# Three list changes at the start of an attention and MLP kernel: pair 7's transposes ahead of unit 5's pieces, unit 10's load behind layer norm's transposes, the first values' casts behind unit 1's keys

## The chip, the cores and the metric

One core of a Trainium2 chip. The metric is device time in microseconds (us) of one execution; most executions of a kernel here agree within 0.3%.

## The reference

Eight batches, 12 heads, 448 rows, head size 64; the attention's output goes through layer norm and an MLP.

```python
q_n, k_n = rmsnorm(q, g_q), rmsnorm(k, g_k)          # over the 64 columns of a head
attn = softmax(q_n @ k_n.T / 8)                      # 448 x 448 per head
x = (attn @ v) as [8, 448, 768]
xn = layernorm(x) * g_ln
out = x + relu(xn @ w_ch1) @ w_ch2                   # 768 -> 3072 -> 768
```

## The kernel before

Heads are worked in pairs (six per batch), and pairs are prepared in units: units 0 and 1 hold one pair, all others two. A unit's preparation is cut into lettered pieces: `a` and `c` square keys and queries (ScalarE), `d` and `e` sum the squares (VectorE), `i`, `j`, `k`, `l`, `m` make the float16 keys `khl` (high and low halves) and queries `qn`, `z` casts the values. Up to unit 7, TensorE then transposes a pair's keys and queries (`K`, `Q`); from unit 8 on this is done by transposing DMA transfers on SyncE's queue (`x`, `y`). Scores are `S`, products with the values `V`, layer norm's transposes `X`.

Batch 0's start is a hand-made list:

```python
ORDER = """
G b0 a0 c0 L4 L5 i0 j0 e0 k0 gq0 l0 b1 m0 a1 c1 K0 Q0 d0 gk0 S0.0 S0.1 i1 e1 d1 z0 g1 j1 l1 m1
k1 b2 ...                                            # cut
S6.6 V6.4 X0 X1 U0 N2 d5 j5 R X2 c5 e5 g5 k5 z5 l5 L7 V6.5 U1 U2 M m5 V6.6
""".split()
DMA_UNIT = 8
```

Everything after it is spread over steps of attention, and the load of unit u + 2 is listed one step behind the last of unit u's evenly spread pieces (step `e`):

```python
            if u < nu - 2 and f"L{u + 2}" not in done:
                todo.setdefault(e + 1, []).append(lambda u=u: self.load_unit(u + 2))
```

What turns out to matter is where a unit's `khl` and `qn` live. They come from a pool with two buffers of each, and the square's result is parked in the same buffer before the keys are made in it:

```python
        self.p_n = pool("p_n", 2)
        ...
            c["qn"] = self.p_n.tile([128, 14, 2, D], FP16, tag="qn", name="qn")[:, 0:g]
            c["khl"] = self.p_n.tile([128, 14, 2, D], FP16, tag="khl", name="khl")[:, 0:g]
        ...
        def square(n):
            o = c["khl" if n == 1 else "qn"].rearrange("p g e d -> p (g e d)").bitcast(FP32)
            ...
            nc.scalar.activation(c["sq", n], c["t"][n], AFT.Square)
        ...
        def dma_k():                                 # from unit 8 on; dma_q likewise reads qn
            nc.sync.dma_start_transpose(
                kU[:, 0:1536].rearrange("p (g c) -> p g c", c=128), khl[:, 0:12])
```

Which of the two buffers a unit gets is not written here; it is settled when the kernel is built.

Of the kernel before, what the change touches and what calls it, by code (L numbers as in the profile page):

```python
# [33 lines left out]


ORDER = """
G b0 a0 c0 L4 L5 i0 j0 e0 k0 gq0 l0 b1 m0 a1 c1 K0 Q0 d0 gk0 S0.0 S0.1 i1 e1 d1 z0 g1 j1 l1 m1
k1 b2 a2 S0.2 d2 c2 S0.3 S0.4 K1 V0.0 e2 i2 S0.5 Q1 g2 l2 S0.6 S1.0 j2 V0.1 S1.1 S1.2 m2 b3
V0.2 a3 V0.3 k2 c3 S1.3 K2 V0.4 S1.4 z2 V0.5 Q2 V0.6 V1.0 S1.5 i3 W0 d3 e3 S1.6 V1.1 V1.2 S2.0
j3 T0 V1.3 S2.1 S2.2 Q3 V1.4 S2.3 K3 S2.4 V1.5 V1.6 S2.5 g3 z3 S2.6 V2.0 S3.0 S3.1 V2.1 k3  # L40
# [1 line left out]
V3.2 d4 i4 K5 W1 c4 W2 V3.3 V3.4 V3.5 V3.6 S4.2 S4.3 V4.0 S4.4 S4.5 V4.1 e4 j4 T1 S4.6 S5.0 k4  # L42
g4 V4.2 V4.3 V4.4 V4.5 S5.1 l4 S5.2 S5.3 K6 V4.6 S5.4 z4 m4 b5 V5.0 S5.5 V5.1 G2 L6 V5.2 S5.6
V5.3 V5.4 V5.5 Q6 a5 i5 V5.6 T3 S6.0 S6.1 S6.2 S6.3 T5 S6.4 A V6.0 V6.1 N0 V6.2 N1 V6.3 S6.5
S6.6 V6.4 X0 X1 U0 N2 d5 j5 R X2 c5 e5 g5 k5 z5 l5 L7 V6.5 U1 U2 M m5 V6.6
""".split()
DMA_UNIT = 8
PE_SET = (DMA_UNIT + 1) % 2
# [27 lines left out]
class _Fast:  # L76
# [381 lines left out]
    def attention(self):  # L458

        n, nu, nb0, done = B * NPAIR, len(UNITS), NPAIR, set(ORDER)  # L460
        todo, last = {}, -9
        for u in range(4, nu):
            p, m = UNIT_PAIR[u], UNITS[u][2]
            st = max(7 * (p - 2 - m) + 2, last + 1, 7 * nb0)
            e = max(7 * (p - 2) - 1, st + 5)
            st, e = EARLY.get(u, (st, e))
            pieces = ["bai", "d", "c", "e", "j", "gv", "k", "l", "m", "w", "x", "y"]
            k = len(pieces) - 2
            if u < DMA_UNIT:
                pieces = pieces[:k]  # L470
            if f"z{u}" in done and u == 4:
                continue
            if u < nu - 2 and f"L{u + 2}" not in done:
                todo.setdefault(e + 1, []).append(lambda u=u: self.load_unit(u + 2))
            last = e
            for x, names in enumerate(pieces):
                at = st + (e - st) * x // (k - 1) if x < k else e + 1 + x - k
                todo.setdefault(at, []).extend(
                    self.prep_ops(u)[y] for y in names
                    if not {y + str(u), f"z{u}" if y in "vw" else ""} & done)  # L480
                if u in (6, 7) and x == 0:
                    todo[at].append(lambda u=u: self.load_w2(u - 6))
        steps, mark = [], [0]

        for p in range(nb0, n + 1):
            for i in range(7):
                c = []
                if i == 0 and p < n and p % NPAIR == 0 and p > nb0:
                    c.append(lambda b=p // NPAIR: self.batch(b))
                c += todo.pop(7 * p + i, [])  # L490
                if p < n and f"S{p}.{i}" not in done:
                    c.append(lambda p=p, i=i: self.scores(p, i))
                if p > nb0:
                    for x in {0: (), 1: (0, 1)}.get(i, (i,)):
                        if f"V{p - 1}.{x}" not in done:
                            c.append(lambda p=p, x=x: self.values(p - 1, x))
                if p > nb0 + 1 and i == 1 and (p - 1) % NPAIR:
                    c.append(lambda p=p: self.stats(p - 2))
                if p + 1 < UNIT_PAIR[DMA_UNIT]:
                    if i == 2 and f"K{p + 1}" not in done:  # L500
                        c.append(lambda p=p: self.trans_k(p + 1))
                    if i == 4 and f"Q{p + 1}" not in done:
                        c.append(lambda p=p: self.trans_q(p + 1))
                if p > nb0 and p % NPAIR == 0 and i == 6:
                    c.append(lambda p=p: self.stats(p - 1))
                if c:
                    steps.append(c)
            if p > nb0 and p % NPAIR == 0:
                mark.append(len(steps))
        return steps, mark  # L510
# [416 lines left out]
```

## Time and profile before

| | before |
|---|---|
| time, median of 3 runs | 615.03 us (614.38 to 616.64) |
| span of the profiled run, granted clock | 613.8 us, 0.996 |
| TensorE busy | 581.6 us (95%) |
| first matmul group of batch 1's MLP (`psH`, 512 columns) | 128.75 us |

In a timeline line the first number is the start in us, the second the busy time, then engine, source line, operation, output and inputs, shapes and count; in brackets stand the engine's idle time just before and what ended it. The prediction shows the lines that it rests on. First ScalarE's timeline of the kernel before at unit 9's two squares:

```profile
110.31 0.95 ACT L215 ACTIVATE khl<-qkv 128x896 f32<-128x896 f32 x1 [1.37 <-PE tr L316]
...
112.72 0.95 ACT L215 ACTIVATE qn<-qkv 128x896 f32<-128x896 f32 x1 [0.42 <-PE tr L330]
```

They are released by TensorE's transposes of pair 13 (unit 7), so unit 9 sits in unit 7's buffers (in the built program the keys of both units stand at address 126848). Then TensorE's timeline of the same stretch, whose only listed gaps from 100 to 128 us are these two:

```profile
111.83 0.35 PE L352 MATMUL psS<-qU,kU 128*128 128x448 f16 x1 [0.27 <-ACT E L358]
...
114.25 0.35 PE L355 MATMUL psS<-qU,kU 128*128 128x448 f16 x1 [0.28 <-ACT E L358]
```

### The profile page before, as it was taken

The numbers are of one execution on the slowest core, as the hardware profiler recorded it, in microseconds if no ns is written. First come the engines' busy times: TensorE is split into PE (matmuls) and PEld (weight loads), VectorE is DVE, ScalarE is ACT, GpSimd is POOL, SyncE is SP. The second block draws the span as 40 slices with busy tenths as digits, with TensorE's granted clock in tenths as the row PEclk, the third lists the DMA queues.
The fourth block names the chain that finished last, engine by engine and source line by source line (L and its number), as shares of the span: only waits on it lengthen the run. The fifth ranks groups of instructions, "written<-read, shape, count | busy, mean of one in ns | idle before, by whom it ended". The sixth has DMA issues, their size and how long they took to land.

```text
span 613.8 us, 11526 instructions
## 1 busy us (share of the span) xinstructions
PE 581.6 (95%) x4500; PEld 346.8 (57%) x4500; DVE 287.2 (47%) x614; ACT 361.4 (59%) x696; POOL 190.1 (31%) x245
## 2 busy tenths in 40 slices
PE   2887999999999999999999999999999999999995
PEld 1555566645566666655566666655566666654564
DVE  5799567823356355643346355642355322440011
ACT  6897886438754498538755398537765377114200
POOL 3844422223452245514453145615322000000000
PEclk9999999999999999999999999999999999999998
DMA  9999899655756477748646496937523330030011
GB/s 213 276 182 229 167 222 204 119 158 122 121 109 126 115 124 152 179 108 143 114 101 140 107 135 151 173 108 149 121 57 87 91 61 2 27 104 0 1 52 56
DMA packets 130861, 75.29 MB, mean 123 GB/s; under 512 B 96656, under 2 KB 121040, under 8 KB 130800
## 3 DMA queue, kind: packets, MB, share of 16 engines
q1 hardware_dynamic: 114048, 45.12, 35.8%
q0 software_dynamic: 16080, 28.94, 21.5%
q8 instruction: 37, 0.61, 0.4%
q10 hardware_dynamic: 672, 0.43, 0.2%
q14 instruction: 24, 0.20, 0.1%
HBM read 52.36 MB, written 11.01 MB: 103 GB/s over the span
## 4 chain that ended last, share of the span: by engine, by line
PE 84%; DMA 5%; DVE 5%; ACT 3%; SPq 1%; issue 1%; POOL 0%; DVEq 0%; ACTq 0%; POOLq 0%
PE psH L611 33%; PE psC L627 33%; PE psS L352 8%; PE oA L381 5%; DMA qkv<-in_k_dram 2%; PE oB L383 2%; ACT E L358 2%; DMA hT<-in_k_dram 1%; PE psS L355 1%; PE psS L356 1%; DVE khl L240 1%; DMA hT<-in_q_dram 1%; ACT qn L215 1%; DVE x L398 1%; DVE qn L67 1%
## 5 line engine op out<-in xcount | busy, mean ns | idle before, releaser
L611 PE MATMUL psH<-xnT,w 128*128 128x512 f16 (+1 forms) x1134 | 242.1, 353 | 1.4 <-DMA xnT<-xn 1.1
L358 ACT ACTIVATE E<-psS,rr_all 128x448 f16<-128x448 f32 x336 | 207.0, 635 | 50.2 <-PE psS L352 44.3
L627 PE MATMUL psC<-w,hT 128*128 128x384 f16 (+1 forms) x1368 | 234.6, 323 | 0.0
L613 ACT ACTIVATE hT<-psH 128x512 f16<-128x512 f32 (+1 forms) x189 | 104.1, 551 | 129.2 <-PE psH L611 126.4
L627 PEld LDWEIGHTS <-hT 128*128 128x128 f16 x1368 | 127.7, 98 | 74.3
L611 PEld LDWEIGHTS <-w 128*128 128x128 f16 x1134 | 102.5, 98 | 82.2 <-issue 2.2
L352 PE MATMUL psS<-qU,kU 128*128 128x448 f16 x288 | 101.5, 359 | 9.1 <-ACT E L358 7.0
L381 PEld LDWEIGHTS <-E 128*128 128x128 f16 x1008 | 71.4, 99 | 50.8 <-issue 5.2
L229 POOL TENSOR_TENSOR qkv<-qkv,gprod 128x896 f32<-128x896 f32 x21 | 43.7, 2079 | 97.7 <-ACT khl L215 62.5
L381 PE MATMUL oA<-v,E 128*128 128x65 f16 x864 | 67.5, 195 | 0.9 <-DVE x L398 0.8
L631 DVE SCALAR_TENSOR_TENSOR x<-psC,rs_all,x 128x384 f32<-128x384 f32 x48 | 29.0, 616 | 70.8 <-PE psC L627 70.2
L396 DVE RECIPROCAL rec_all<-oA 128x6 f32<-128x6 f32 x48 | 9.3, 194 | 98.1 <-PE oA L381 98.0
L383 PE MATMUL oB<-v,E 128*128 128x65 f16 x288 | 52.2, 194 | 0.1
L127 POOL DMA_DIRECT2D qkv<-in_k_dram x14 | 11.2, 797 | 131.1 <-ACT E L358 69.2
L218 DVE TENSOR_REDUCE ssq<-khl 128x14 f32<-128x896 f32 (+1 forms) x24 | 25.6, 1065 | 45.6 <-ACT khl L215 45.5
L352 PEld LDWEIGHTS <-kU 128*128 128x128 f16 x288 | 28.3, 99 | 24.2 <-issue 5.9
L218 DVE TENSOR_REDUCE ssq<-qn 128x14 f32<-128x896 f32 (+1 forms) x25 | 26.2, 1047 | 23.0 <-ACT qn L215 22.8
L67 DVE SCALAR_TENSOR_TENSOR qn<-qkv,rq 128x256 f16<-128x256 f32 (+1 forms) x72 | 26.9, 431 | 19.3 <-ACT rq L223 19.3
L383 PEld LDWEIGHTS <-E 128*128 128x128 f16 x336 | 32.7, 97 | 0.5 <-DVE xl L403 0.2
L398 DVE TENSOR_TENSOR x<-oA,rec_all 128x384 f32<-128x384 f32 x48 | 26.8, 558 | 1.7 <-DVE rec_all L397 0.2
L240 DVE TENSOR_TENSOR khl<-qkv,khl 128x896 f16<-128x896 f32 x21 | 22.8, 1084 | 7.9 <-ACT khl L237 7.9
L540 DVE BATCH_NORM_STATS2 stat<-x 128x6 f32<-128x256 f32 x72 | 26.1, 415 | 0.7
(104 smaller groups left out, 449.0 us busy)
## 6 DMA issues: line engine op xcount, KB each, us to landing
out_dram<-x SPq DMA_DIRECT2D x20, 384.0 KB, 2.5
qkv<-in_k_dram POOLq DMA_DIRECT2D x14, 384.0 KB, 3.9
qkv<-in_q_dram POOLq DMA_DIRECT2D x14, 384.0 KB, 5.1
qkv<-in_v_dram POOLq DMA_DIRECT2D x14, 384.0 KB, 6.7
w<-in_moe_w_ch_dram POOLq DMA_DIRECT2D x3, 1536.0 KB, 13.0
w<-in_moe_w_ch_dram POOLq DMA_DIRECT2D x2, 2304.0 KB, 23.7
qkv<-in_k_dram SPq DMA_DIRECT2D x7, 384.0 KB, 5.7
qkv<-in_q_dram SPq DMA_DIRECT2D x7, 384.0 KB, 5.0
```

Of the source, the lines that this page charges most:

```text
L67: nc.vector.scalar_tensor_tensor(out=out, in0=x, scalar=8.0, in1=r.unsqueeze(2).broadcast_to([x.shape[0], g, D]), op0=ALU.mult, op1=ALU.mult)
L218: nc.vector.tensor_reduce(out=c["ssq"][:, n], in_=c["sq", n], axis=AX.X, op=ALU.add)
L229: (nc.vector if u in DVE_KG else nc.gpsimd).tensor_tensor(out=c["t"][1], in0=c["t"][1], in1=sh.gprod.unsqueeze(1).broadcast_to([128, g, D] ...
L352: nc.tensor.matmul(ps[:, 0:S], c["main"][:, ts(i, 128)], q[:, ts(h, S)], start=True, stop=True)
L358: nc.scalar.activation(out=c["E"][:, i], in_=ps[:, 0:S], func=AFT.Exp, scale=self.rr[:, g:g + 1], bias=EXP_BIAS)
L381: nc.tensor.matmul(oA[:, t, cs], E[:, i, ts(t, 128)], rhs, start=(i == 0 and t == 0), stop=(i == 6 and t == 2))
L383: nc.tensor.matmul(oB[:, cs], E[:, i, 320:448], rhs, start=(i == 0), stop=(i == 6))
L398: nc.vector.tensor_tensor(out=x[:, :, 128 * hp:128 * hp + 128].rearrange("p t (e d) -> p t e d", e=2), in0=oA[:, :, :, 0:D], in1=rec[:, 0: ...
L611: nc.tensor.matmul(ps[:, 0:N], sh.w1[:, dc, ts(f, 128)], xnT[:, dc, 0:N], start=(dc == 0), stop=(dc == NDC - 1))
L613: nc.scalar.activation(out=hT[:, f, 0:N], in_=ps[:, 0:N], func=AFT.Relu)
L627: nc.tensor.matmul(ps[:, 0:g[1]], hT[:, f, ts(t, 128)], sh.w2[:, f, cols], start=(f == 0), stop=(f == NFF - 1))
L631: nc.vector.scalar_tensor_tensor(out=x[:, cols], in0=ps[:, 0:g[1]], scalar=self.rs[:, b, t:t + 1], in1=x[:, cols], op0=ALU.mult, op1=ALU.add)
```

## The change

It is meant to take three waits away from the first 128 us: that of unit 1's keys behind the values' casts, that of pair 7's transposes behind unit 5's pieces, and that of layer norm's transposes behind unit 10's load in SyncE's queue.

```diff
-G b0 a0 ... i1 e1 d1 z0 g1 j1 l1 m1
+G b0 a0 ... i1 e1 d1 g1 j1 l1 m1 z0
 ...
-S6.6 V6.4 X0 X1 U0 N2 d5 j5 R X2 c5 e5 g5 k5 z5 l5 L7 V6.5 U1 U2 M m5 V6.6
+S6.6 V6.4 X0 X1 U0 N2 d5 j5 R X2 K7 Q7 c5 e5 g5 k5 z5 l5 L7 V6.5 U1 U2 M m5 V6.6
 ...
-                todo.setdefault(e + 1, []).append(lambda u=u: self.load_unit(u + 2))
+                todo.setdefault(e + (8 if u == DMA_UNIT else 1), []).append(
+                    lambda u=u: self.load_unit(u + 2))
```

More of the change, by code (lines that the diff above doesn't have):

```diff
@@ L36 @@
 ORDER = """
-G b0 a0 c0 L4 L5 i0 j0 e0 k0 gq0 l0 b1 m0 a1 c1 K0 Q0 d0 gk0 S0.0 S0.1 i1 e1 d1 z0 g1 j1 l1 m1
+G b0 a0 c0 L4 L5 i0 j0 e0 k0 gq0 l0 b1 m0 a1 c1 K0 Q0 d0 gk0 S0.0 S0.1 i1 e1 d1 g1 j1 l1 m1 z0
 k1 b2 a2 S0.2 d2 c2 S0.3 S0.4 K1 V0.0 e2 i2 S0.5 Q1 g2 l2 S0.6 S1.0 j2 V0.1 S1.1 S1.2 m2 b3
```

## The prediction

> **What bounds the kernel now.** I read the page first: busy times per engine, then the rows of 40 slices.
>
> ```profile
> PE 581.6 (95%) x4500; PEld 346.8 (57%) x4500; DVE 287.2 (47%) x614; ACT 361.4 (59%) x696; POOL 190.1 (31%) x245
> ...
> PE   2887999999999999999999999999999999999995
> ...
> ACT  6897886438754498538755398537765377114200
> ```
>
> TensorE is busy 581.6 of 613.8 us. Its 32 us of idle time lie almost wholly at the left end. The busy time by stretches (windows) says how much is where: TensorE was busy 4.28 us of the first 17, 28.86 of the 35 up to 52, 7.97 of the 10 up to 62, 62.32 of the 66 up to 128, and 478.21 of the last 486 (nearly all of that idle is the tail after the last matmul). From 128 us on, a stall-free queue of fixed work runs to the end. So whatever brings TensorE to that point earlier comes off the time one for one, and nothing else can. The time is about 128 + 486, and only the 128 is open to this change.
>
> Next, the waits. On POOL's timeline at the start, the first casts of the values hold up the cast of unit 1's keys, since they wait for a load until 13.69:
>
> ```profile
> 13.69 1.15 POOL L285 CAST v<-w 128x768 f16<-128x768 f32 x1 [9.37 <-DMA w<-in_v_dram]
> 14.78 0.64 POOL L291 CAST vl<-w 64x128 f16<-64x128 f32 x2
> 15.48 0.56 POOL L235 CAST khl<-hT 128x448 f16<-128x448 f32 x1
> ```
>
> VectorE and ScalarE then show what hangs on that cast: the subtraction that makes the low half of the keys, TensorE's transpose K1 (17.08), and the next exp, which TensorE is too late for:
>
> ```profile
> 16.08 0.95 DVE L240 TENSOR_TENSOR khl<-hT,khl 128x448 f16<-128x448 f32 x1 [1.93 <-POOL khl L235]
> ...
> 18.64 0.63 ACT L358 ACTIVATE E<-psS,rr_all 128x448 f16<-128x448 f32 x1 [1.80 <-PE psS L352]
> ```
>
> From 18.64 to 52 ScalarE has no gap over 0.7 us (its waits there: 0.39, 0.61, 0.41), so this stage is bound by ScalarE's fixed list of exps and squares, and starts when this wait ends.
>
> The third group is TensorE's own gaps after 58 us, from its timeline:
>
> ```profile
> 57.86 1.14 PE L611 MATMUL psH<-xnT,w 128*128 128x384 f16 x6 [0.34 <-ACT hT L661]
> 61.52 0.22 PE L327 MATMUL tr<-id,qn 128*128 128x128 f16 x1 [1.16 <-DVE kU L318]
> 66.21 0.35 PE L352 MATMUL psS<-qU,kU 128*128 128x448 f16 x1 [0.83 <-ACT E L358]
> 99.82 0.25 PE L381 MATMUL oA<-v,E 128*128 128x65 f16 x3 [0.82 <-DVE x L398]
> 128.75 1.46 PE L611 MATMUL psH<-xnT,w 128*128 128x512 f16 x6 [1.06 <-DMA xnT<-xn]
> ```
>
> The last is the start of batch 1's MLP. SyncE's queue shows why xnT is late: unit 10's load stood in it for 8.7 us for its buffer, then issued until 109.5, and the transposes of unit 8 and LN came behind it:
>
> ```profile
> 103.98 0.37 SPq L127 DMA_DIRECT2D qkv<-in_k_dram  x1
> ...
> 109.57 3.36 SPq L258 DMA_TRANSPOSE kU<-khl  x1
> ...
> 122.08 5.23 SPq L586 DMA_TRANSPOSE xnT<-xn  x4
> ```
>
> **What the Trainium skill says.** "PSUM — Partial Sum Buffer", section Engine vs sequencer instructions: the ScalarE, VectorE and GpSimd queues are strict FIFO. The trace agrees: unit 1's cast started right behind the two value casts, though its inputs were ready at about 12.3 (the ssq reduction that reads the same tile started at 11.70 and took 0.61). "SBUF — State Buffer", section SBUF: two separate sides: GpSimd and a VectorE operation with two SBUF inputs lock a shared port pair, and the later blocks. The trace fits: the subtraction above took 0.95 us beside a POOL copy, against 0.62 for unit 0's same form alone. "TensorE: Matmul & The Clock Gate", Part 1: the clock is halved until about 3.4 us of sustained activity. Here a 448-column score matmul took 0.53 to 0.58 us up to 24 us and 0.35 from 25.8 on. "DMA: Bandwidth & Descriptors", Queues, rings and completion order: each DMA engine goes round between the queues it has work for. Here the weight load on the software queue took 89% of the engines from 48 to 56 us and the SyncE queue 22%, so unit 6's keys landed 11.2 us after issue.
>
> **Part 1, value casts behind unit 1's keys.** Nothing is added; POOL's order becomes key cast, q copy, then the three value casts. The key cast can run at 12.36 to 12.92. VectorE finishes unit 1's qn at 14.15 and subtracts at once, ending between 14.75 and 15.3 (port lock). K1's transposes then start near 15.1 instead of 17.08. The value casts follow the q copy: 14.7 (or 15.25 behind the lock) plus 0.8 for the first, so the first value matmuls can go at about 16.1, just behind K1. The next score comes at 16.4 and its exp at 16.84, when ScalarE is free of the one before, instead of 18.64: 1.8 us. Further on the q reduction ends near 18.0 instead of 19.70, and unit 2's subtraction starts near 20.1 instead of 21.70, as POOL's product for unit 2 cannot move (POOL's sum of work is the same): 1.6 us. From there ScalarE's list carries it. The loads of weights move along, as POOL issues them after its products. I take **-1.6**.
>
> **Part 2, pair 7's transposes (K7, Q7) ahead of unit 5.** Now they stand in the MLP stream; Q7 waits 1.16 us, because VectorE copies K7 out only at 60.81, behind unit 5's five pieces and an evacuation. After, they follow LN's third transpose X2 directly, all through the one PSUM tile `tr`. In the before clock: X2's copy ends at 55.83, so K7 starts 0.85 late; its copy ends near 57.05, so Q7 starts 0.8 late; then V6.5, the first up matmuls until 59.6, and the first psH near 60.3 after a 0.45 wait for ScalarE. The third psH starts at 62.24 against 61.91: **+0.3**. One stall becomes two of similar sum.
>
> But pacing changes too. Without K7 and Q7 two steps of attention are empty and vanish (44 steps instead of 46 in batch 0), so unit 6's pieces start at the first psH instead of the third, and the scores of pair 7 one chunk earlier. ScalarE, which idled 0.46, 0.88 and 2.19 us from 58 to 63, starts its squares sooner. I followed both lists to 66.8 us: the 0.83 stall at 66.21 becomes about 0.5 near 64.6, and TensorE is then ahead by one score (0.19), so **-0.5** from that point. Last, VectorE's list as built has changed near 98 us: pair 9's evacuation now precedes unit 8's subtraction (1.09 us at 97.68), which is what the 0.82 stall at 99.82 waited behind. I count **-0.8** for it and **+0.5** for new waits of this kind that I cannot see in the reshuffled stretch.
>
> **Part 3, unit 10's load behind LN.** SyncE drops 5.5 us of issue and the 8.7 us buffer wait. Unit 8's eight transposes (12.2 us of issue) then end near 111 instead of 122; LN's four issue as their xn arrive (the last ends at 121.83): issued by 123.1, landed 2.55 later at 125.7, while TensorE has work until 127.69. The stall goes: **-1.06**, I count -1.0. The load itself follows the stores, from about 129.5 to 135; unit 10's first piece comes nine steps of some 1.6 us later, near 143, and keys landed in 5.7 us at the median for SyncE. Hidden.
>
> Sum: -1.6 +0.3 -0.5 -0.8 +0.5 -1.0 = -3.1, so 615.03 becomes about **612.0 us**.
>
> **Rivals.** (a) The start's gain is lost again, because the stage to 56 us is bound by transfers: DMA is at 90% or more up to about 60 us, and the weight stream ended at 56.2. For it: those digits. Against: TensorE and ScalarE never waited for a load between 18.6 and 56. If so only parts 2 and 3 count: 613.6. (b) ScalarE, in order, meets unit 6's square before its keys have landed (near 57), or the reshuffled order makes new exp waits; then psH stalls behind it. For it: the pieces come 3 us earlier against a load that took 11.2. Against: by my count the square stands near 60 even with the shift. Cost 1 to 3 us: 613 to 615. (c) The two serial copies in `tr` cost more than the one wait: with VectorE late, K7 and Q7 lose 2.5 instead of 1.65: 612.9. (d) The clock gate opens one window sooner since TensorE starts K1 earlier, saving up to another 1 us: 611. (e) The load of unit 10 is now late for its square: then a wait near 143; I see 5 us of slack.
>
> **Range and chances.** All terms are local and small against 2% (12.3 us). Losing the start's gain and adding one stall of rival b gives 614.4; everything at its best, with d and no new waits, gives 609.8. Range **609.8 to 614.4**. Chances: faster by over 2%: 0.01; within 2%: 0.98; slower: 0.01.
>
> **What will show it.** POOL's first cast is khl near 12.4 and K1 stands near 15.1; the exp at 18.64 is near 16.9 (part 1 right). TensorE shows two gaps of about 0.8 us ahead of K7 and Q7, with none of 1.16 later (part 2). The 0.82 wait for x and the 1.06 wait for xnT are gone, and no psH or square waits for unit 6 or unit 10 (part 3). Batch 1's first psH starts near 125.6 instead of 128.75, and the 486 us behind it are unchanged. I am wrong if that stretch after the first psH of batch 1 changes by more than 0.5 us, or if a new wait over 1 us stands between 52 and 125.

## The result, and the profile after

The changed kernel took 615.17 us (median of 4 runs, 614.83 to 615.97), the kernel before 615.08 us beside it (4 runs, 614.38 to 616.64). The ratio is 1.000, with a 95% interval of 0.9978 to 1.0022: the same, and outside the predicted range of 609.8 to 614.4. A ratio here is the mean time of one kernel's fast runs over that of the other's fast runs of the same rounds, so it is not quite the ratio of the medians quoted.

The three waits did go. Here is the start of the changed kernel, from the timeline of all engines:

```profile
12.71 0.56 POOL L235 CAST khl<-hT 128x448 f16<-128x448 f32 x1 [8.40 <-DVE ssq L218]
...
14.33 0.62 DVE L240 TENSOR_TENSOR khl<-hT,khl 128x448 f16<-128x448 f32 x1
...
15.96 1.87 ACT L358 ACTIVATE E<-psS,rr_all 128x448 f16<-128x448 f32 x3
```

The key cast stands at 12.71 in place of 15.48, the subtraction takes 0.62 in place of 0.95 us (it starts first here, and now the copy of queries on GpSimd that starts beside it takes 0.89 us in place of 0.56), and the exp that waited 1.80 us at 18.64 is the third of an unbroken group. TensorE's timeline of the changed kernel:

```profile
54.71 0.22 PE L313 MATMUL tr<-id,khl 128*128 128x128 f16 x1 [0.71 <-DVE xnT L599]
...
56.01 0.22 PE L327 MATMUL tr<-id,qn 128*128 128x128 f16 x1 [0.75 <-DVE kU L318]
...
64.28 0.35 PE L352 MATMUL psS<-qU,kU 128*128 128x448 f16 x1 [0.59 <-ACT E L358]
...
110.36 0.35 PE L352 MATMUL psS<-qU,kU 128*128 128x448 f16 x1 [1.83 <-ACT E L358]
...
111.52 0.22 PE L327 MATMUL tr<-id,qn 128*128 128x128 f16 x1 [0.69 <-DVE kU L318]
...
114.27 0.35 PE L355 MATMUL psS<-qU,kU 128*128 128x448 f16 x1 [0.92 <-ACT E L358]
...
127.54 1.46 PE L612 MATMUL psH<-xnT,w 128*128 128x512 f16 x6
```

Up to 107 us it goes as planned: two waits of 0.7 us for one of 1.16, a stall of 0.59 for 0.83, none of 0.82 at 100; layer norm's wait ahead of 127.54 is gone too. But three new stalls, 3.44 us in all, stand from 108 to 114 us, where the kernel before had 0.55. They wait for exps and for a copy of keys, and ScalarE's timeline shows what held those up:

```profile
108.83 0.95 ACT L215 ACTIVATE khl<-qkv 128x896 f32<-128x896 f32 x1 [2.84 <-DMA kU<-khl]
...
112.74 0.95 ACT L215 ACTIVATE qn<-qkv 128x896 f32<-128x896 f32 x1 [1.91 <-DMA qU<-qn]
```

Unit 9's squares now wait for DMA transfers that *read* `khl` and `qn`: unit 8's transposes. SyncE's queue, whose transposes in the kernel before began at 109.57:

```profile
98.62 3.12 SPq L258 DMA_TRANSPOSE kU<-khl  x1
...
104.39 4.63 SPq L268 DMA_TRANSPOSE qU<-qn  x3
...
119.35 5.20 SPq L587 DMA_TRANSPOSE xnT<-xn  x4
124.64 4.08 SPq L669 DMA_DIRECT2D out_dram<-x  x4
128.81 0.85 SPq L127 DMA_DIRECT2D qkv<-in_k_dram  x1
```

With the load out of the way they are issued 11 us earlier, and they land slowly. In the view of DMA issues from 97 to 130 us (last column: median us from issue to landing) the changed kernel has

```profile
qU<-qn SPq DMA_TRANSPOSE x5, 3.3
...
kU<-khl SPq DMA_TRANSPOSE x3, 5.7
```

where both take 2.4 us in the kernel before. In all ten profiles the weights on GpSimd's software queue run until some point between 102.6 and 105.6 us. In the four whose key transposes start beside them (97.6 to 98.7 us) the keys' median is 4.8 to 6.7 us; in the six whose transposes start after them it is 2.4 to 2.6. No run separates this from other differences.

The builds say why the square waits for them at all. These are the waits of the square of unit 9's keys, as built, in the kernel before and the changed one. DMAHW stands for transfers from SyncE's queue; DMAHW1 to DMAHW3 in the changed build are unit 8's three key transposes; DMAHW0, and all three in the build before, are unit 9's own load:

```
before:  Activation khl<-qkv  waits DMAHW1, DMAHW2, DMAHW0, PE
changed: Activation khl<-qkv  waits DMAHW2, DMAHW1, DMAHW3, DMAHW0, DVE
```

PE stood for unit 7's buffer; with unit 8's transposes in its place, unit 9 has been given unit 8's buffer (address 123264 for the keys of both units). VectorE's list has changed along: the sum of unit 9's squared keys now precedes the copy of pair 13's keys, so that copy waits too. Among eleven builds of mine, the four without the load's move (before, part 1, part 2, both) give unit 9 the buffer of unit 7, and all seven with it (in three of them the load or unit 8's transposes were listed at another step) give it that of unit 8. Six of the eleven are before, changed, noload, loadonly, casts, pair7.

### The profile page after: what moved, and what is told of

Its sections match the earlier page's. It is cut to its first block, busy times and chain, and to the rows that moved or that the text cites. A ratio compares the mean times of both kernels' runs of the same rounds, so it can differ in the third digit from the quotient of the medians.

```text
span 613.6 us, 11527 instructions
## 1 busy us (share of the span) xinstructions
PE 581.0 (95%) x4500; PEld 346.7 (57%) x4500; DVE 286.4 (47%) x614; ACT 361.0 (59%) x696; POOL 188.1 (31%) x245
## 4 chain that ended last, share of the span: by engine, by line
PE 84%; ACT 2%; SPq 1%; DVE 1%; issue 1%; DMA 0%; DVEq 0%; ACTq 0%
PE psH L612 34%; PE psC L628 34%; PE psS L352 7%; PE oA L381 5%; PE oB L383 2%; PE psS L355 1%; PE psS L356 1%; SPq L268 1%; ACT E L358 1%; ACT qn L215 1%; SPq L261 0%; DMA qU<-qn 0%; DVE qn L67 0%; SPq L271 0%; DVE x L398 0%
## 5 line engine op out<-in xcount | busy, mean ns | idle before, releaser
L229 POOL TENSOR_TENSOR qkv<-qkv,gprod 128x896 f32<-128x896 f32 x21 | 43.7, 2080 | 98.7 <-issue 49.7
```

Of the source, the lines that this page charges most:

```text
L229: (nc.vector if u in DVE_KG else nc.gpsimd).tensor_tensor(out=c["t"][1], in0=c["t"][1], in1=sh.gprod.unsqueeze(1).broadcast_to([128, g, D] ...
```

## The experiments

Two calls of four kernels each. The kernel before ran beside them: 614.74 us (median of 11 runs) in the first call, 614.44 (11 runs) in the second. I read the profiled runs between marks, since their starts differ by chance (more on this below the table). K0 is TensorE's first transpose; A is VectorE's start on the `xn` group of batch 0 (50.93 in the kernel before); B its second combination of a down-projection result with the residual (108.24); C its start on the `xn` group of batch 1 (118.09); D its last such operation ahead of batch 1's MLP (127.73); E the first `psH` of batch 1 (128.75, on TensorE); then the end of the span. All in us:

| run | K0 to A | A to B | B to C | C to D | D to E | E to end | ratio (95%) | time against before |
|---|---|---|---|---|---|---|---|---|
| before | 42.36 | 57.31 | 9.85 | 9.64 | 1.02 | 485.0 | | |
| changed | 40.91 | 55.41 | 13.17 | 9.41 | -0.21 | 486.1 | 1.000 (0.9978-1.0022) | 0.0 |
| again | 40.97 | 55.42 | 13.92 | 9.40 | -0.20 | 485.6 | 1.0015 (1.0002-1.0027) | +0.9 |
| fixslot | 41.06 | 55.41 | 9.89 | 9.64 | -0.20 | 485.0 | 0.9940 (0.9927-0.9953) | -3.7 |
| noload | 39.87 | 55.42 | 9.89 | 9.64 | 1.34 | 485.0 | 0.9957 (0.9943-0.9971) | -2.6 |
| loadonly | 41.04 | 57.31 | 11.77 | 11.08 | -0.20 | 485.6 | 1.0037 (1.0022-1.0051) | +2.3 |
| casts | 39.87 | 57.31 | 9.85 | 9.64 | 0.20 | 485.1 | 0.9979 (0.9967-0.9992) | -1.3 |
| pair7 | 41.56 | 55.41 | 9.89 | 9.64 | 1.03 | 485.0 | 0.9979 (0.9966-0.9991) | -1.3 |
| pad2 | 42.34 | 57.31 | 9.85 | 9.64 | 0.68 | 485.6 | 1.0013 (1.0000-1.0026) | +0.8 |
| swap | 41.18 | 57.31 | 21.00 | 11.95 | -0.21 | 484.6 | 1.0166 (1.0151-1.0180) | +10.2 |

The last column is the ratio's distance from 1 times the time of before in that call. From A to B the runs fall into two values without any scatter, 57.31 without part 2 and 55.4 with it. K0 to A is not so clean: runs with the same lists up to A differ by up to 1.3 us. This goes with the granted clock. In the trace's clock records the full clock begins at 25.58 and 25.50 us in before and pad2 (42.36 and 42.34 us from K0 to A), but at 19.75 to 21.29 in loadonly, swap and pair7 (41.04 to 41.56). It begins for good at 24.20 to 25.24 in changed, again and fixslot (40.91 to 41.06), but at 19.16 and 19.77 in noload and casts (39.87 both). So a profile's own start holds about 1 us of chance.

**again** is the changed kernel once more, unedited, in five rounds.

> The changed kernel once more, in more rounds, for a tight interval and to see whether its end takes longer each time. Slot theory (unit 9's keys and queries were given the buffers that unit 8's transposing transfers still read, so ScalarE's two squares wait 2.8 and 1.9 us and TensorE loses about 2.9 us there): the two waits are there again, within 0.3 us of those sizes; time 615.0 +- 0.5, ratio to before 0.999 to 1.001. Rival (the gain is lost at the end of the program, where the profiled run took 1 us longer behind the last normalised product): the VectorE semaphore operation to final drain gap is again 2.6 us in this run, against 0.1 us before.

It took 615.49 us (6 runs). The squares waited 3.43 and 2.07 us, the first more than 0.3 us above the first profile (unit 8's first key transpose took 10.2 us to land, where it had taken 8.2), and TensorE's three stalls came to 4.18 us (2.42, 0.69, 1.07). The ratio, 1.0015, is just above the expected 0.999 to 1.001. The end was longer again, too, so the rival holds a part; pad2 below is about that.

**fixslot** names the two buffers by the unit's parity. The same edit on the kernel before builds the identical program, so it changes nothing but the choice; on the changed kernel it leaves TensorE's order of work as it is and gives unit 9 unit 7's buffers. VectorE's order at unit 9 goes back with it, to the copy ahead of the sum of squares; swap, below, separates the two.

```diff
-            c["qn"] = self.p_n.tile([128, 14, 2, D], FP16, tag="qn", name="qn")[:, 0:g]
-            c["khl"] = self.p_n.tile([128, 14, 2, D], FP16, tag="khl", name="khl")[:, 0:g]
+            c["qn"] = self.p_n.tile([128, 14, 2, D], FP16, tag=f"qn{u % 2}", name="qn", bufs=1)[:, 0:g]
+            c["khl"] = self.p_n.tile([128, 14, 2, D], FP16, tag=f"khl{u % 2}", name="khl", bufs=1)[:, 0:g]
```

> The changed kernel with unit u's khl and qn buffers named by u % 2, so unit 9 gets unit 7's, as in the kernel before; TensorE's list, 10,700 rows, is the same as the changed kernel's. Slot theory: both squares of unit 9 no longer wait for a transfer; the 1.83, 0.69 and 0.92 us stalls between 110 and 115 us shrink to the 0.3 to 0.6 us that before has in all; the first psH of batch 1 comes 3 to 4 us ahead of before's 128.75 (124.8 to 125.8), and the time is 611.0 to 612.2, 3 to 4 us under before. Rival A (the lead is eaten anyway between 115 and 128 by layer norm's transposes, which wait for the load or for the residual's last product): the first psH stays at 127 to 128 and the time at 614 to 615. Rival B (loss at the end): time stays within 0.5 of the changed kernel though the first psH moves.

It took 611.30 us (5 runs). ScalarE's timeline:

```profile
107.31 0.95 ACT L215 ACTIVATE khl<-qkv 128x896 f32<-128x896 f32 x1 [1.29 <-DMA kU<-khl]
...
109.73 0.95 ACT L215 ACTIVATE qn<-qkv 128x896 f32<-128x896 f32 x1 [0.42 <-PE tr L330]
```

The idle times are those of before (1.37, 0.42). The label DMA in the first line misleads: as built, this square waits for TensorE and its own load, and it starts at 107.31 together with VectorE's copy of the same TensorE transposes; several semaphores end here at nearly the same time. TensorE's stalls between 108 and 114 us are 0.27 and 0.28 again, and the first `psH` comes at 124.53, slightly ahead of what I expected. This is the fastest kernel. This fits the slot theory, and rivals A and B are out; whether the buffer or VectorE's order did it is left to swap.

**noload** leaves out part 3 only.

> The changed kernel without its third part: unit 10's load is listed where it was. In its build unit 9 has unit 7's buffers. Slot theory (the load move alone flips the buffers): no transfer wait in front of unit 9's squares; TensorE's lead of about 3 us at 107 lives on to 115; layer norm's wait of about 1.06 us stays; first psH of batch 1 at 125.5 to 126.5, time 612.0 to 613.0. Rival A (the waits come from the earlier queries and keys of pair 7 and the pacing, not from the load): waits of 2 us at unit 9's squares, time 615 to 616. Rival B (the load, still ahead of layer norm's transposes on SyncE, takes no part in the lead): layer norm's wait grows to 3 to 4 us and the time is 614.5 to 615.5.

It took 611.77 us (6 runs). Unit 9's squares waited 1.29 and 0.42 us, both for TensorE. The time is 0.2 us below the expected range, and the first `psH` comes 0.9 us ahead of it, at 124.64; this profile is one of those with an early clock. Layer norm's wait is there, as TensorE's timeline shows, with 1.37 us instead of 1.06, so of rival B little is left:

```profile
124.64 1.46 PE L611 MATMUL psH<-xnT,w 128*128 128x512 f16 x6 [1.37 <-DMA xnT<-xn]
```

So parts 1 and 2 alone bring 2.6 us, and adding part 3 takes it all back and 0.9 more: from 0.9957 to 1.0015. With the buffers fixed, part 3 adds 1.0 us of gain (0.9957 to 0.9940).

**loadonly** is part 3 on the kernel before.

> The third part alone: before with unit 10's load behind layer norm's transposes. In its build unit 9 takes unit 8's buffers. Slot theory: waits for unit 8's transposes of 2 to 3 us at unit 9's two squares, stalls of 2 to 3.5 us on TensorE between 109 and 118, about 1.1 us back at layer norm: 615.5 to 617, that is +0.5 to +2 over before. Rival (the load move is worth its 1 us, and the wait arises only with the lead of the two other parts): no stall over 0.6 us there, time 614.0 to 614.4.

It took 616.84 us (6 runs), slower than before. Here only the queries' square waited; ScalarE's timeline:

```profile
107.63 0.94 ACT L215 ACTIVATE khl<-qkv 128x896 f32<-128x896 f32 x1
...
113.20 0.95 ACT L215 ACTIVATE qn<-qkv 128x896 f32<-128x896 f32 x1 [3.27 <-DMA qU<-qn]
```

I had expected both. Unit 8's first key transpose started at 97.60 and took 9.3 us to land, so it was done by 106.9, just ahead of the keys' square. The stall on TensorE was 2.39 us ahead of 114.72, and something came on top which I had not expected: from C to D this run takes 11.08 us in place of 9.64. The table of windows gives the granted clock (the third value from the right; the two behind it are the DMA share and GB/s):

```profile
112.00:114.70 2.70, 0.34 (x6) 0.19 (x4) 0.52 (x1) 1.50 (x3) 0.83 (x1) 1.00 0.06 12
114.70:117.00 2.30, 2.27 (x12) 1.22 (x12) 2.21 (x6) 1.86 (x3) 0.59 (x2) 0.63 0.00 0
117.00:119.00 2.00, 2.00 (x9) 0.95 (x8) 1.97 (x10) 0.09 (x1) 0.00 (x0) 0.57 0.00 0
119.00:121.00 2.00, 2.00 (x14) 1.22 (x13) 2.00 (x3) 0.34 (x2) 0.00 (x0) 1.00 0.00 0
```

The clock was halved from 115.32 to 118.73 us, behind the stall. In `again` a stall of 2.42 us did not do that (1.00 throughout). The clock records suggest why. Within a trace they lie whole multiples of 3.41 us apart, which makes a grid of intervals. The stall of loadonly fell into one interval (111.91 to 115.32, 2.39 us idle); in `again` a boundary at 109.88 cut it, and no interval there held more than 1.75 us of listed stalls. So part of this run's size is the chance of where the stall falls; that the load's move alone makes the wait, without any lead of the other parts, is shown.

**casts** is part 1 alone, **pair7** part 2 alone.

> The first part alone: the first values' casts behind unit 1's keys, in GpSimd's list only. Theory (the parts add up, about 1.4 us each for the casts and the rest, as long as unit 9 keeps unit 7's buffers, which this build does): the second K transposes come 1.5 us earlier, the layer norm's first transposes 1.4 us earlier, and all of it lives to the end: ratio 0.9972 to 0.9982, 613.0 to 613.7. Rival (the casts' gain is swallowed later by the pacing of batch 0): ratio 0.999 to 1.001.

> The second part alone: pair 7's transposes ahead of unit 5's late pieces. In its build unit 9 keeps unit 7's buffers. Theory: the keys' and queries' transposes wait about 0.7 us each, the 0.83 us stall at 66 turns into 0.6, the 0.82 us stall at 100 goes, so TensorE is ahead by about 1.5 us at the tenth down product and stays so: ratio 0.9972 to 0.9985, 613.0 to 613.9. Rival (the second part brings nothing by itself and needs the first one's lead): ratio 0.9992 to 1.001.

They took 612.46 us (6 runs) and 612.98 us (5 runs), just under the expected times; the ratios, which are taken against before, are in the expected ranges. Each is 0.21% under before; together 0.42%, and noload, which holds both, has 0.43%. The parts add up. From K0 to A the five profiles with part 1 average 40.54 us (39.87 to 41.06) and the five without it 41.70 (41.04 to 42.36): 1.2 us for part 1. With like clocks it is 1.3 to 1.4 (the five profiles whose full clock begins for good at 24 us or later) and 1.2 (casts against loadonly). From A to B part 2 brings 1.90 us. Of this, TensorE's listed stalls account for 1.1 (5.29 to 4.18 us) and its busy time between the marks for 0.7 (51.83 to 51.14; why it falls isn't shown).

**pad2** tests the longer end. In the trace's records of the last instructions, VectorE's closing semaphore operation and its drain, which the final barrier waits for, stand as follows (us from the span's start):

```
          VectorE instructions   semaphore    drain    779th instruction
before             780             611.05     611.16        613.42
changed            782             610.12     612.70        612.70
again              782             610.56     612.95        612.95
loadonly           782             611.93     614.39        614.39
fixslot            781             606.84     606.95        609.19
noload             780             606.89     607.00        609.22
pad2               782             610.56     612.91        612.91
swap               779             622.33     622.44        624.70
```

Changed, again and loadonly have two more semaphore operations on VectorE than before, fixslot one more, swap one fewer; pad2 adds two tiny clears of a small tile to the kernel before, at the start.

```diff
-        nc.vector.memset(self.rs, RS_LO)
+        nc.vector.memset(self.rs, RS_LO); nc.vector.memset(self.rs, RS_LO); nc.vector.memset(self.rs, RS_LO)
```

> The kernel before with two more 64-byte clears of a small tile in VectorE's setup, nothing else: its VectorE list gets as long as the changed kernel's (782 instructions for 780). Tail theory (in the three profiles with 782 instructions VectorE's last drain comes 2.4 to 2.6 us behind its semaphore operation and delays the final barrier, with 780 or 781 it comes 0.1 us behind, so the length of the list sets where a pause of VectorE falls): from the last normalised product to the end 7.1 to 7.6 us in place of 6.5, ratio 1.0005 to 1.0015. Rival (the longer end belongs to what changed at unit 9, or is chance): 6.4 to 6.6 us, ratio 0.9995 to 1.0005.

It took 615.15 us (5 runs), a ratio of 1.0013 whose interval just reaches 1. Its drain comes 2.35 us behind the semaphore operation, as in the changed kernel, and from the last product to the end it needs 7.08 us, against 6.56 before and 7.57, 7.11 and 7.12 in the three others with 782 instructions. (The 7.08 is a hair below the expected 7.1.) So the length of VectorE's list decides where a pause at its end falls, and it costs 0.5 to 1.0 us in the profiles. The last column shows more: the pause is in all ten profiles (casts and pair7 too), and it is always the 779th instruction that starts 2.3 to 2.6 us behind that semaphore operation. With 782 instructions the 779th is the drain that the final barrier waits for; with fewer it comes after that drain. What the pause is stays open. Each trace has a 16 KB transfer of the kind `instruction` that starts within 0.7 us of that semaphore operation, so a fetch of instructions is a candidate, but no run tests it.

**swap** is the kernel before with no part of the change, but from unit 9 on the buffers are named the other way round.

```diff
+            ... tag=f"qn{(u + (u > 8)) % 2}", name="qn", bufs=1)
+            ... tag=f"khl{(u + (u > 8)) % 2}", name="khl", bufs=1)
```

> The kernel before, with no part of the change, but from unit 9 on the khl and qn buffers are named the other way round, so unit 9 takes unit 8's. Unit 8's transposes stand behind unit 10's load on SyncE here and are issued from 109.6 to 122 us. Slot theory: ScalarE's square of unit 9's keys waits for them until 117 to 120 us, its queries' until 121 to 124, TensorE loses 7 to 11 us, ratio 1.011 to 1.018. Rival (who waits at unit 9 does not matter, the loss in the changed kernel comes from the order on VectorE, where the sum of squares stands ahead of the copy of pair 13's keys): VectorE's order is unchanged here, so under 1 us, ratio 0.999 to 1.0015.

It took 624.45 us (4 runs). ScalarE's timeline:

```profile
115.92 0.95 ACT L215 ACTIVATE khl<-qkv 128x896 f32<-128x896 f32 x1 [7.91 <-DMA kU<-khl]
...
122.45 0.95 ACT L215 ACTIVATE qn<-qkv 128x896 f32<-128x896 f32 x1 [4.53 <-DMA qU<-qn]
```

The keys' square starts a little earlier than I expected, the loss of 10.2 us is in the expected range, and the rival (VectorE's order alone) is out: that order is the one of before here, with the sum of squares behind the copy. With fixslot, the slot theory is shown. This is the same cause in a larger dose, without the change. Some of it is the clock again: TensorE stalled 6.80 us from 110.65 on, the granted clock was 0.50 from 112.69 to 129.76, the next 448-column score took 0.53 us in place of 0.35, and C to D took 11.95 us in place of 9.64.

## Why the prediction was wrong

Taken step by step, against the marks:

1. **Where a gain counts.** Right in the main: the queue behind E runs without stalls in every profile. The 486 us behind E are not quite fixed, though: 484.6 to 485.1 with 779 to 781 instructions on VectorE, 485.6 to 486.1 with 782. The prediction allowed 0.5, so one of its signs of being wrong came up here (1.0 us in the changed kernel).
2. **Part 1, -1.6.** The mechanism was right to the line. The size was 1.2 to 1.4 by the marks and 1.3 by the time of casts.
3. **Part 2, +0.3 -0.5 -0.8 = -1.0.** The mechanism was right (two waits of 0.7, the stall at 66 smaller, the one at 100 gone). The size was 1.90 by the marks and 1.3 (0.6 to 2.1) by the time: I had followed the pacing only to 66.8 us and had not counted on TensorE's busy time falling by 0.7.
4. **Part 3, -1.0.** The direct gain is right: D to E goes from 0.20 to 1.34 (mean 0.85) in the five profiles with the load ahead (swap, whose batch 1 is late for another reason, apart) to -0.20 in all with it behind, 1.05 us. Unit 8's transposes ended near 111, as I wrote.
5. **"+0.5 for new waits of this kind that I cannot see in the reshuffled stretch."** This term failed, and with it the claim that part 3 costs nothing. I gave the term to part 2 and to VectorE's order; the wait belonged to part 3, at ScalarE's two squares of unit 9, which wait for unit 8's transposes. It measured 3.3 us from B to C in the changed kernel and 4.1 in `again`, less 0.2 from C to D, and the longer end added 1.0 and 0.6 from E on: 4.1 and 4.4 together in place of 0.5. Removing both (fixslot) moves the ratio from 1.0015 to 0.9940, 4.6 us. The prediction's other sign of being wrong, a new wait over 1 us between 52 and 125, came too: TensorE's 1.83 us ahead of 110.36.

With the measured sizes the sum is -1.2 -1.9 -1.05 +3.1 +1.0 = -0.05 for the changed kernel's profile and -1.2 -1.9 -1.05 +3.8 +0.6 = +0.25 for that of `again`; 0.0 and +0.9 (interval 0.1 to 1.7) were measured. The changed kernel's three parts are worth 3.7 us, a little more than the 3.1 that I predicted, and the build's other choice of buffer, with the longer end, gave it back.

Rival b named the right kind of wait ("the reshuffled order makes new exp waits", 1 to 3 us) but looked for it at unit 6's load. Rival d's effect is there in about its size (1 us from K0 to A with an early clock), but with and without part 1, so by chance. I had also stated that no square would wait for unit 6 or unit 10, which is so; I had not asked about unit 9, and had seen in part 3 that unit 8's transposes would run from 99 to 111 instead of 110 to 122 without asking who wants the tiles that they read. That the builder gives a unit whichever buffer it expects to come free first, and that earlier transposes tip this, is my reading of eleven builds; it isn't shown by a run. That the buffer is the cause is shown, by fixslot in one direction and swap in the other.

## What to carry to other kernels

A transfer that is moved in a queue moves everything behind it, and what reads a tile earlier may also decide who gets that tile next: compare the built waits of the instructions that reuse its buffers, not only the order. Where a rotating pool feeds slow readers, such as transposing transfers, beside quick ones, name the buffer of each user explicitly; here it cost no memory and made the change worth 0.6% in place of nothing. Before looking for a lost gain on the bounding engine, follow its new stalls back one engine at a time: here from TensorE to exps, from these to a square, from the square to a transfer that only read.

## What the Trainium skill lacked or had wrong

- "TensorE: Matmul & The Clock Gate", Part 1, has the clock halved after at least one idle window of about 3.4 us. The grid of 3.41 us in the clock records agrees, but the window need not be idle throughout. In swap the clock fell to 0.50 at 112.69, 2.04 us into a stall, and in loadonly 2.39 us of stall within one interval were enough (0.50 from 115.32 to 118.73). In the changed kernel and in `again`, intervals with 1.52 and 1.75 us of listed stalls left it at 1.00.
- "DMA: Bandwidth & Descriptors", DMA Transpose (X-bar), gives the constraints of such transposes, but no time from issue to landing. Here it was a median of 2.4 to 2.6 us for the keys where the software queue's weights had ended, and 4.8 to 6.7 us where they still ran; that queue took 24.6% of the engines while unit 8's transposes were issued in the changed kernel (98.5 to 111.7 us).
- No page names the pause of VectorE at the end of a program: its 779th instruction started 2.3 to 2.6 us behind the closing semaphore operation in all ten profiles. With 782 instructions that was the drain ahead of the final barrier; with 779 to 781 the drain came 0.1 us behind.
